# Softmax by small exponentials on ScalarE, and another order of the first batch, in a fused attention and expert kernel

## The chip, the cores and the metric

The kernel runs on one core of a Trainium2 chip. A core has a matrix engine (TensorE, PE in the profile), a vector engine (VectorE, DVE), an activation engine (ScalarE, ACT), a general engine (GpSimd, POOL) and SyncE (SP), which issues the DMAs. Each engine runs its own instructions in their order and waits for the others by semaphores. The metric is the device time of one execution in microseconds (us): 1990.22 before, the median of three runs (1989.96 to 1992.01).

## The reference

Three layers follow each other, all in float32. The change touches the first.

```python
def _attn_ref(q, k, v):                       # 4 batches, 8 heads, 576 rows, 64 wide
    k_p = k.reshape(B, H, 72, 8, D).mean(axis=3)
    v_p = v.reshape(B, H, 72, 8, D).mean(axis=3)
    scores = scale * np.matmul(q, k_p.transpose(0, 1, 3, 2))
    scores = scores - np.max(scores, axis=-1, keepdims=True)
    attn = np.exp(scores)
    attn = attn / (np.sum(attn, axis=-1, keepdims=True) + 1e-09)
    return np.matmul(attn, v_p)
# x: (2304, 512), the heads side by side
# _moe_ref:  8 experts, x -> relu(x @ w1[e]) @ w2[e], summed with weights P[:, e]
#            from x @ w_gate by 8 rounds of row and column normalisation
# _moe2_ref: (silu(x @ w_gate) * (x @ w_val)) @ w_out
```

## The kernel before

Products of float32 are made of three products of a high and a low part (`mm3`, L112): a high part is a copy by ScalarE, a low part the difference to it by VectorE or POOL. The attention stage takes the first 200 us or so; the experts and the gated layer fill the rest.

**Tiles.** The 576 rows of a batch are cut into five query tiles (four of 128 rows, one of 64), 20 in all. For each, `task_a` transposes the queries (TensorE, then a copy qT by ScalarE, L345), `task_b` makes the scores of 8 heads by 72 keys in a PSUM tile mps (four products, L353) and has VectorE take the maximum of each head (L359) and the difference of scores and maximum into a tile e (L360). `task_exp` is one exponential over all 576 columns by ScalarE (L367). `task_b2` sums each head (L373, VectorE), adds a small constant, inverts (L374, L375) and multiplies (L377, on POOL, for tiles 1 and 2 on VectorE). `task_c` transposes e and splits it into aTh (ScalarE, L405) and aTl (VectorE, L406). When two (or three) tiles of a batch are through, `task_d` multiplies them with the masked values vh and vl in two halves of four heads, each in its own mps tile, and splits the result into xh and xl (L421, L422).

**Keys and values.** Rows of eight are summed by VectorE or POOL. `key_blocks` copies the transposed keys into block form kbd, the upper half of the partitions by ScalarE, the lower half by the engine it is given. `task_v2` splits the values; `mask` multiplies them with a head mask, vh on POOL, vl on VectorE (L324).

**Expert units in the gaps.** As soon as 256 rows of x are there, nine units of the first expert group are queued (`group0_units`): four first-layer blocks (12 products into a PSUM tile hps, then a copy hh by ScalarE, L135, and a low part hl by VectorE, L136), one gate block, four second-layer units. `fill()` puts one of them into the order at hand.

**What sets the order.** It is written out by hand (L605 to L694): what stands in the code first is issued first on each engine. A loop step takes one tile: query tile i+3, a unit, `task_c(i)`, a unit, `task_b(i+2)`, a unit, `task_exp`, keys and values of the next batch, and at the end of a chunk `values(i)`. PSUM has eight banks: two for tiles y, two for tiles h (queries, first-layer and gate blocks), and two mps tiles of two banks each. A new tile waits until the tile that had its banks before is read. TensorE's first 16 products (`warm`) multiply the identity with itself and are not used.

Loads go out on SP in the order of the code. A key or value tile kv has five buffers (NKV), so the first batch's values wait until the first keys are summed.

## Time and profile before

| | |
|---|---|
| median of three runs | 1990.22 us |
| profiled execution, its own time | 1990.33 us |
| its span in the profile | 1988.6 us |
| PE busy | 1964.8 us (99%) |
| DVE busy | 1425.2 us (72%) |
| ACT busy | 885.1 us (45%) |
| POOL busy | 1305.7 us (66%) |

A row of a timeline or of the chain gives the start and the length in us; in square brackets stands how long the engine was idle before it and who released it. "x8" is the number of records; a float32 product that is not split has two of them. PEclk is the clock that TensorE was granted, as a share of its full 2.4 GHz.

### The profile page before, as it was taken

How to read it: one execution, taken by the hardware profiler on the slowest of the kernel's cores; microseconds unless marked ns; L12 is line 12 of the kernel's file. 1: busy time of each engine (PE TensorE's matmuls, PEld its weight loads, DVE VectorE, ACT ScalarE, POOL GpSimd, SP SyncE). 2: the span in 40 equal slices, each digit the busy share in tenths (PEclk: the TensorE clock that was granted, in tenths of full speed). 3: DMA queues.
4: the chain of work that ended last, by engine and by line, in shares of the span. 5: the costliest groups of instructions: out<-in, count | busy, mean ns of one | idle time of the engine just before them, and what ended most of it. 6: DMA issues, size and time to landing. Idle time of an engine off the chain costs nothing.

```text
span 1988.6 us, 31110 instructions
## 1 busy us (share of the span) xinstructions
PE 1964.8 (99%) x11067; PEld 1872.2 (94%) x11067; DVE 1425.2 (72%) x2258; ACT 885.1 (45%) x1707; POOL 1305.7 (66%) x1162
## 2 busy tenths in 40 slices
PE   8999999999999999999999999999999999999998
PEld 7899888999999899999999999999999999999997
DVE  7773868777777868777777788777776855656555
ACT  4453534444444443443444434444444554544542
POOL 5775567878888466867767667677675766445442
PEclk8999999999999999999999999999999999999999
DMA  6674677888888889988989889899988564544532
GB/s 180 190 212 117 196 283 266 308 305 296 314 305 308 309 307 315 333 304 307 315 307 312 299 305 332 313 309 313 309 318 289 174 238 149 200 160 138 179 139 85
DMA packets 217227, 513.82 MB, mean 258 GB/s; under 512 B 35472, under 2 KB 107760, under 8 KB 210928
## 3 DMA queue, kind: packets, MB, share of 16 engines
q1 hardware_dynamic: 212176, 496.10, 72.7%
q0 software_dynamic: 4896, 15.73, 2.9%
q8 instruction: 88, 1.44, 0.3%
q14 instruction: 67, 0.55, 0.1%
HBM read 360.73 MB, written 151.04 MB: 257 GB/s over the span
## 4 chain that ended last, share of the span: by engine, by line
PE 91%; DVE 4%; POOL 2%; issue 2%; ACT 1%; DMA 0%; SPq 0%; DVEq 0%; POOLq 0%; ACTq 0%
PE aps L116 8%; PE aps L114 8%; PE aps L115 8%; PE mbs L114 7%; PE mbs L115 7%; PE mbs L116 7%; PE yps L1157 6%; PE yps L1159 6%; PE yps L1158 6%; PE cps L114 4%; PE cps L116 4%; PE cps L115 4%; PE bps L114 2%; PE bps L115 2%; PE bps L116 2%
## 5 line engine op out<-in xcount | busy, mean ns | idle before, releaser
L1086 ACT COPY LF<-aps 128x384 f32<-128x384 f32 x378 | 181.3, 480 | 440.4 <-PE aps L116 438.4
L1318 POOL TENSOR_TENSOR LR<-LF,LR 128x384 fp32r<-128x384 f32 x240 | 260.6, 1108 | 173.3 <-ACT LR L1316 173.0
L114 PE MATMUL mbs<-LR 128*128 128x384 f32 x840 | 283.2, 337 | 0.0
L115 PE MATMUL mbs<-LR 128*128 128x384 f32 x840 | 282.5, 336 | 0.0
L1365 DVE TENSOR_TENSOR AC<-mbs,AC 128x768 f32<-128x768 f32 x196 | 187.2, 955 | 132.4 <-PE mbs L116 131.7
L116 PE MATMUL mbs<-LR 128*128 128x384 f32 x840 | 281.9, 336 | 0.0
L1157 PE MATMUL yps<-LR 128*128 128x512 f32 x576 | 225.7, 392 | 0.3 <-DVE AC L1417 0.3
L1159 PE MATMUL yps<-LR 128*128 128x512 f32 x576 | 225.1, 391 | 0.6 <-DVE LR L1600 0.6
L1158 PE MATMUL yps<-LR 128*128 128x512 f32 x576 | 224.6, 390 | 0.2 <-POOL LR L66 0.2
L835 POOL TENSOR_TENSOR LR<-praw,LR 128x512 fp32r<-128x512 f32 (+1 forms) x130 | 136.1, 1068 | 108.1 <-ACT LR L829 63.0
L835 POOL TENSOR_TENSOR LR<-sums,LR 128x1024 fp32r<-128x1024 f32 x65 | 158.8, 2444 | 68.3 <-ACT LR L829 68.3
L1331 POOL TENSOR_TENSOR LF<-LF 128x384 f32<-128x384 f32 x120 | 128.9, 1074 | 56.5 <-DVE LF L1485 44.8
L115 PEld LDWEIGHTS mbs<-LR 128*128 128x128 f32 x840 | 157.8, 188 | 0.0
L116 PEld LDWEIGHTS mbs<-LR 128*128 128x128 f32 x840 | 157.7, 188 | 0.0
L114 PEld LDWEIGHTS mbs<-LR 128*128 128x128 f32 x840 | 157.6, 188 | 0.0
L1419 DVE SCALAR_TENSOR_TENSOR AC<-yps,pr,AC 128x512 f32<-128x512 f32 x168 | 121.3, 745 | 30.7 <-PE yps L1159 27.0
L1325 ACT COPY LF<-bps 128x384 f32<-128x384 f32 x120 | 57.7, 481 | 185.3 <-DVE bps L1485 179.8
L1335 POOL TENSOR_TENSOR LF<-LF 128x384 f32<-128x384 f32 x120 | 130.5, 1088 | 9.4
L1159 PEld LDWEIGHTS yps<-LR 128*128 128x128 f32 x576 | 108.1, 188 | 24.5 <-DVE LR L1600 1.0
L1157 PEld LDWEIGHTS yps<-LR 128*128 128x128 f32 x576 | 108.2, 188 | 19.1 <-DVE AC L1417 0.7
L66 POOL TENSOR_TENSOR LR<-rraw,LR 128x512 fp32r<-128x512 f32 x72 | 99.2, 1399 | 41.0 <-ACT LR L65 36.6
L1158 PEld LDWEIGHTS yps<-LR 128*128 128x128 f32 x576 | 108.2, 188 | 18.4 <-POOL LR L66 0.7
(308 smaller groups left out, 5744.1 us busy)
## 6 DMA issues: line engine op xcount, KB each, us to landing
LR<-w1s_d SPq DMA_DIRECT2D x210, 512.0 KB
LR<-w2s_d SPq DMA_DIRECT2D x210, 512.0 KB
w1s_d<-LR SPq DMA_DIRECT2D x29, 1792.0 KB
w2s_d<-LR SPq DMA_DIRECT2D x24, 1024.0 KB
w2s_d<-LR SPq DMA_DIRECT2D x90, 256.0 KB
praw<-in_moe_w_dram SPq DMA_DIRECT2D x30, 512.0 KB
rraw<-in_moe_w_dram SPq DMA_DIRECT2D x30, 512.0 KB
LR<-rows_d POOLq DMA_DIRECT2D x12, 1024.0 KB, 7.0
```

The lines of the kernel that those rows point to most:

```text
L114: nc.tensor.matmul(ps, lhsT=wh, rhs=ah, start=start, stop=False, skip_group_check=more)
L115: nc.tensor.matmul(ps, lhsT=wh, rhs=al, start=False, stop=False, skip_group_check=more)
L116: nc.tensor.matmul(ps, lhsT=wl, rhs=ah, start=False, stop=stop, skip_group_check=more)
L835: nc.gpsimd.tensor_tensor(out=lo, in0=src, in1=hi.bitcast(F32), op=ALU.subtract)
L1086: nc.scalar.copy(out=t, in_=ps[:, :HB])
L1157: nc.tensor.matmul(ps, lhsT=hh[:, o:o + P], rhs=wh, start=j == 0, stop=False)
L1158: nc.tensor.matmul(ps, lhsT=hh[:, o:o + P], rhs=wl, start=False, stop=False)
L1159: nc.tensor.matmul(ps, lhsT=hl[:, o:o + P], rhs=wh, start=False, stop=j == 1)
L1318: eng.tensor_tensor(out=lo[:, c], in0=src[:, c], in1=hi[:, c].bitcast(F32), op=ALU.subtract)
L1331: nc.gpsimd.tensor_tensor(out=r_of(q, a), in0=r_of(q, b), in1=r_of(q, a), op=ALU.subtract)
L1335: nc.gpsimd.tensor_tensor(out=r_of(q, a), in0=r_of(q, a), in1=r_of(q, b), op=ALU.subtract)
L1365: nc.vector.tensor_tensor(out=acc_of(m), in0=ps[:, :, :HB], in1=acc_of(m), op=ALU.add)
```

## The change

The scores keep their PSUM tile. VectorE takes the negated maximum only. ScalarE runs one exponential for each head of a tile, eight of 72 columns, from PSUM, with the negated maximum as bias and the sum of the head as its accumulated output; the scale goes into the copy of the queries. The difference and the sum by VectorE are gone. In the loop the first four exponentials come before a unit and the other four behind it. The key blocks of the first batch are copied by columns: ScalarE both partition halves of the first two blocks, VectorE those of the last two. The first batch's values are loaded into the accumulator AC, which is not in use then. Its four masks are all made on POOL and stand before the transposes. Seven more unused products stand before the first transposes. The second half of the first chunk's value products goes to two y tiles instead of an mps tile. Tile 2 is normalised on POOL. The low parts of the first expert's weights are made in two instructions each.

```diff
@@ -98,8 +98,11 @@
             if kind == "col":
                 hi, lo = (a.rearrange("p (k f) -> p k f", k=KD) for a in (hi, lo))
             load_w(src + 1)
-            raw = raws[src]
-            split(raw[:, :, j * P:(j + 1) * P] if kind == "col" else raw[:, j, :], hi, lo)
+            raw = raws[src][:, :, j * P:(j + 1) * P] if kind == "col" else raws[src][:, j, :]
+            nc.scalar.activation(out=hi, in_=raw, func=AF.Copy)
+            for c in range(2):
+                h = (slice(None), slice(2 * c, 2 * c + 2)) if kind == "col" else (slice(None), slice(2 * P * c, 2 * P * c + 2 * P))
+                nc.gpsimd.tensor_tensor(out=lo[h], in0=raw[h], in1=hi[h].bitcast(F32), op=ALU.subtract)
             if j == 1:
                 load_w(src + 3)
             parts.append((hi, lo))
@@ -247,7 +250,10 @@
 
         flat = src[b].rearrange("h (j r) d -> (h j) (r d)", r=POOL)
         r = min(P, NK - c * P)
-        t = att.tile([P, POOL * D], F32, tag="kv", name="kv", bufs=NKV)
+        if src is v and b == 0:
+            t = AC[:, c * POOL * D:(c + 1) * POOL * D]
+        else:
+            t = att.tile([P, POOL * D], F32, tag="kv", name="kv", bufs=NKV)
         nc.sync.dma_start(out=t[:r], in_=flat[c * P:c * P + r])
         kv_t[src is k, b, c] = t
 
@@ -280,16 +286,16 @@
         r = min(P, NK - c * P)
         nc.tensor.transpose(flat[:, c * P:c * P + r], kp[:r, c].rearrange("p a d -> p (a d)"), ident[:r, :r])
 
-    def key_blocks(flat, second):
+    def key_blocks(flat, a, copy):
         keys = flat[:, 0:NK].rearrange("p (a b) -> p a b", a=NP)
-        nc.scalar.copy(out=kbd[0:D, :, 0:SP], in_=keys[0:D, :, 0:SP])
-        second(out=kbd[D:P, :, SP:2 * SP], in_=keys[D:P, :, SP:2 * SP])
+        copy(out=kbd[0:D, a, 0:SP], in_=keys[0:D, a, 0:SP])
+        copy(out=kbd[D:P, a, SP:2 * SP], in_=keys[D:P, a, SP:2 * SP])
 
     def task_k2(b):
         flat = m_tile().rearrange("p a b -> p (a b)")
         for c in range(NC):
             key_transpose(flat, c)
-        key_blocks(flat, nc.scalar.copy)
+        key_blocks(flat, slice(0, NP), nc.scalar.copy)
 
     def first_keys():
 
@@ -299,7 +305,8 @@
             if c == 3:
                 query(0)
             key_transpose(flat, c)
-        key_blocks(flat, nc.vector.tensor_copy)
+        key_blocks(flat, slice(0, 2), nc.scalar.copy)
+        key_blocks(flat, slice(2, NP), nc.vector.tensor_copy)
 
     vh = att.tile([P, 2, NP, 2, D], F32R, name="vh")
     vl = att.tile([P, 2, NP, 2, D], F32R, name="vl")
@@ -324,13 +331,13 @@
         eng.tensor_tensor(out=dst[:, s, :, a], in0=src[:, s:s + NP].to_broadcast([P, NP, 2 - s, D]),
                           in1=hmask[:, s, :, a].unsqueeze(3).to_broadcast([P, NP, 2 - s, D]), op=ALU.mult)
 
-    def task_v2(b):
+    def task_v2(b, eng=nc.vector):
 
         nc.scalar.activation(out=vp_h, in_=vp, func=AF.Copy)
         nc.vector.tensor_tensor(out=vp_l, in0=vp, in1=vp_h.bitcast(F32), op=ALU.subtract)
         for s in range(2):
             mask(nc.gpsimd, vh, vp_h.bitcast(F32), s)
-        return [lambda s=s: mask(nc.vector, vl, vp_l, s) for s in range(2)]
+        return [lambda s=s: mask(eng, vl, vp_l, s) for s in range(2)]
 
     qT, ex, aT = {}, {}, {}
 
@@ -342,7 +349,7 @@
             nc.tensor.transpose(ps[:, p * P:p * P + n],
                                 t[:n, 2 * p:2 * p + 2, :].rearrange("p a d -> p (a d)"), ident[:n, :n])
         qt = att.tile([P, NP, P], F32, tag="qT", name="qT", bufs=2)
-        nc.scalar.copy(out=qt[:, :, :n], in_=ps.rearrange("p (a t) -> p a t", a=NP)[:, :, :n])
+        nc.scalar.mul(out=qt[:, :, :n], in_=ps.rearrange("p (a t) -> p a t", a=NP)[:, :, :n], mul=1.0 / (POOL * D ** 0.5))
         qT[i] = qt
 
     def task_b(i):
@@ -356,24 +363,23 @@
         st = att.tile([P, 3, 2, 4, 1], F32, tag="st", name="st", bufs=3)
         e = e_bufs[i % 3]
         ev = e[:n, 0:NK].rearrange("p (a h j) -> p a h j", a=2, h=4)
-        nc.vector.tensor_reduce(out=st[:n, 0, :, :, 0], in_=sc, axis=AX.X, op=ALU.max)
-        nc.vector.tensor_tensor(out=ev, in0=sc, in1=st[:n, 0].to_broadcast([n, 2, 4, SP]), op=ALU.subtract)
-        ex[i] = (e, st)
-
-    def task_exp(i):
+        nc.vector.tensor_reduce(out=st[:n, 0, :, :, 0], in_=sc, axis=AX.X, op=ALU.max, negate=True)
+        ex[i] = (e, st, sc, ev)
+
+    def task_exp(i, which=(0, 1)):
         n = per[i][2]
-        e = ex[i][0]
-
-        nc.scalar.activation(out=e[:n, 0:NK], in_=e[:n, 0:NK], func=AF.Exp, scale=1.0 / (POOL * D ** 0.5))
+        e, st, sc, ev = ex[i]
+        for a in which:
+            for h in range(4):
+                nc.scalar.activation(out=ev[:, a, h], in_=sc[:, a, h], func=AF.Exp, bias=st[:n, 0, a, h, :],
+                                     accum_out=st[:n, 1, a, h, :])
 
     def task_b2(i):
         b, s, n = per[i]
-        e, st = ex[i]
-        ev = e[:n, 0:NK].rearrange("p (a h j) -> p a h j", a=2, h=4)
-        nc.vector.tensor_reduce(out=st[:n, 1, :, :, 0], in_=ev, axis=AX.X, op=ALU.add)
+        e, st, sc, ev = ex[i]
         nc.vector.tensor_scalar(out=st[:n, 1], in0=st[:n, 1], scalar1=EPS, scalar2=None, op0=ALU.add)
         nc.vector.reciprocal(out=st[:n, 2], in_=st[:n, 1])
-        eng = nc.vector if i in (1, 2) else nc.gpsimd
+        eng = nc.vector if i == 1 else nc.gpsimd
         eng.tensor_tensor(out=ev, in0=ev, in1=st[:n, 2].to_broadcast([n, 2, 4, SP]), op=ALU.mult)
 
     CH = [(0, 2), (2, TPB)]
@@ -396,7 +402,7 @@
         if key not in aT:
             aT[key] = [att.tile([P, NC, 320], F32R, tag=t, name=t, bufs=1) for t in ("aTh", "aTl")]
         ah, al = aT[key]
-        e, st = ex.pop(i)
+        e = ex.pop(i)[0]
         ps = m_tile()
         flat = ps.rearrange("p a b -> p (a b)")
         for c in range(NC):
@@ -409,17 +415,21 @@
     def task_d(b, c, half):
         s0, cn = chunk_rows(b, c)
         ah, al = aT[b, c]
-        ps = m_tile()
+        ps = [new_y().unsqueeze(1) for _ in range(2)] if b + c == 0 and half else [m_tile()]
         for pp in range(2):
             p = half * 2 + pp
+            y = ps[pp][:, 0, :cn] if len(ps) == 2 else ps[0][:, pp, :cn]
             for s in range(2):
                 wh = vh[:, s, p].rearrange("p a d -> p (a d)")
                 wl = vl[:, s, p].rearrange("p a d -> p (a d)")
-                mm3(ps[:, pp, :cn], wh, wl, ah[:, p + s, :cn], al[:, p + s, :cn], s == 0, s == 1)
+                mm3(y, wh, wl, ah[:, p + s, :cn], al[:, p + s, :cn], s == 0, s == 1)
         t0 = b * S + s0
-        dst = (slice(None), slice(half * 2, half * 2 + 2), slice(t0, t0 + cn))
-        nc.scalar.activation(out=xh[dst], in_=ps[:, :, :cn], func=AF.Copy)
-        nc.vector.tensor_tensor(out=xl[dst], in0=ps[:, :, :cn], in1=xh32[dst], op=ALU.subtract)
+        w = 2 // len(ps)
+        for i, y in enumerate(ps):
+            k = half * 2 + i * w
+            dst = (slice(None), slice(k, k + w), slice(t0, t0 + cn))
+            nc.scalar.activation(out=xh[dst], in_=y[:, :, :cn], func=AF.Copy)
+            nc.vector.tensor_tensor(out=xl[dst], in0=y[:, :, :cn], in1=xh32[dst], op=ALU.subtract)
 
 
     def task_gate(j):
@@ -617,13 +627,13 @@
         for c in range(NC - 1):
             task_v1(0, c)
         last_values()
+        warm(7)
         task_b2(0)
         task_b2(1)
-        masks.extend(task_v2(0))
+        for f in task_v2(0, nc.gpsimd):
+            f()
         task_c(0)
         task_c(1)
-        next_mask()
-        next_mask()
         query(2)
         split_w(2)
         query(3)
@@ -633,11 +643,11 @@
         task_exp(2)
         split_w(4)
         task_b2(2)
-        gate_weights()
         fill()
         query(4)
         task_b(3)
         fill()
+        gate_weights()
         task_exp(3)
         split_w(6)
         for bc in key_parts(3):
@@ -663,9 +673,10 @@
                     task_k2(t // TPB)
                     fill()
                 task_b(t)
+                task_exp(t, (0,))
                 fill()
                 next_mask()
-                task_exp(t)
+                task_exp(t, (1,))
             for bc in key_parts(t):
                 task_k1(*bc)
             for bc in value_parts(i):
```

ScalarE in the first batch, from the key blocks to the split of the values; first before, then after.

```order
L285 COPY kbd<-mps 64x4x72
L345 COPY qT<-qps 128x512
L367 ACTIVATE e_110<-e_110 128x576
L367 ACTIVATE e_111<-e_111 128x576
L320 COPY vp<-yps 128x64
L329 ACTIVATE vp_h<-vp 128x320
```

```order
L291 COPY kbd<-mps 64x2x72
L292 COPY kbd<-mps 64x2x72
L352 ACTIVATE qT<-qps 128x512
L374 ACTIVATE e_110,st<-mps,st 128x72 x8
L374 ACTIVATE e_111,st<-mps,st 128x72 x8
L327 COPY vp<-yps 128x64
L336 ACTIVATE vp_h<-vp 128x320
```

Two exponentials have become sixteen, which read the scores (mps) and the maxima (st) and write the sums into st; two key copies of half the columns stand where one stood.

TensorE at the same place, from the scores of tiles 0 and 1 to those of tile 2; first before, then after.

```order
L353 MATMUL mps<-kbd,qT 128x144 x8
L318 MATMUL yps<-kv,ident 128x64 x8
L403 MATMUL mps<-ident,e_110 128x128 x5
L403 MATMUL mps<-ident,e_111 128x128 x5
L342 MATMUL qps<-ident,q 128x128 x8
L353 MATMUL mps<-kbd,qT 128x144 x4
```

```order
L360 MATMUL mps<-kbd,qT 128x144 x8
L325 MATMUL yps<-AC,ident 128x64 x8
L613 MATMUL mps<-ident 128x128 x7
L409 MATMUL mps<-ident,e_110 128x128 x5
L409 MATMUL mps<-ident,e_111 128x128 x5
L349 MATMUL qps<-ident,q 128x128 x8
L360 MATMUL mps<-kbd,qT 128x144 x4
```

The seven unused products stand between the sum of the last values and the transposes of tile 0.

ScalarE in the loop at tile 7 (its exponentials write e_111), where first-layer copies hh surround them; first before, then after.

```order
L135 ACTIVATE hh<-hps 128x256
L405 ACTIVATE aTh<-mps 128x5x128
L135 ACTIVATE hh<-hps 128x256 x2
L367 ACTIVATE e_111<-e_111 128x576
L345 COPY qT<-qps 128x4x64
L135 ACTIVATE hh<-hps 128x256
```

```order
L138 ACTIVATE hh<-hps 128x256
L411 ACTIVATE aTh<-mps 128x5x128
L138 ACTIVATE hh<-hps 128x256
L374 ACTIVATE e_111,st<-mps,st 128x72 x4
L138 ACTIVATE hh<-hps 128x256
L374 ACTIVATE e_111,st<-mps,st 128x72 x4
L352 ACTIVATE qT<-qps 128x4x64
L138 ACTIVATE hh<-hps 128x256
```

The copy hh that stood before the exponential now stands behind four of the eight.

## Rows read from the trace of the kernel before

**Rows 1.** The page, busy time: us, share of the span, instructions
```profile
PE 1964.8 (99%) x11067; PEld 1872.2 (94%) x11067; DVE 1425.2 (72%) x2258; ACT 885.1 (45%) x1707; POOL 1305.7 (66%) x1162
```

**Rows 2.** Windows of TensorE: from:to, length, busy (instructions), granted clock, DMA share, GB/s
```profile
17.00:18.00 1.00, 0.06 (x1) 1.00 1.16 231
...
18.00:19.00 1.00, 0.00 (x0) 0.52 0.34 64
...
24.00:25.00 1.00, 1.00 (x6) 0.57 0.39 94
```

**Rows 3.** Waits of TensorE, 30 to 260 us: sum, times, longest
```profile
PE hps L114 <- DVE hl L136: 2.9, 4, 1.1
```

**Rows 4.** Chain of waits, 10 to 28 us: start, length, what
```profile
10.77 0.47 DVE kbd L286
...
11.28 2.30 PE mps L353 x8
...
13.61 0.77 DVE st L359
...
17.62 0.20 DVE st L375
...
19.42 1.33 DVE e L377
...
20.88 1.31 PE mps L403 x5
...
23.77 2.03 DVE vl L324 x2
```

**Rows 5.** Timeline of TensorE: start, length, instruction, idle before and releaser
```profile
25.25 0.38 PE L114 MATMUL mps<-aTh,vh 128*128 128x256 f32 x1
...
27.41 0.36 PE L114 MATMUL mps<-aTh,vh 128*128 128x256 f32 x1 [0.46 <-DVE e L360]
...
30.47 0.38 PE L115 MATMUL hps<-xl,wh 128*128 128x256 f32 x1 [0.34 <-DVE xl L422]
...
32.64 0.38 PE L114 MATMUL hps<-xh,wh 128*128 128x256 f32 x1
...
54.24 0.42 PE L114 MATMUL mps<-aTh,vh 128*128 128x320 f32 x1 [0.81 <-DVE aTl L406]
```

**Rows 6.** ScalarE by line and shape, whole run: busy, mean ns, idle before
```profile
L367 ACT ACTIVATE e<-e 128x576 f32<-128x576 f32 x16 | 10.9, 683 | 16.0 <-DVE e L360 15.8
...
L65 ACT ACTIVATE wh<-raw 128x512 fp32r<-128x512 f32 x8 | 4.6, 621 | 0.0
...
L894 ACT ACTIVATE pr<-pr,small 128x144 f32<-128x144 f32 x1 | 0.4, 418 | 0.6 <-DVE small L893 0.6
...
L320 ACT COPY vp<-yps 128x64 f32<-128x64 f32 x1 | 0.2, 193 | 0.0
```

**Rows 7.** VectorE by line and shape, 0 to 200 us
```profile
L360 DVE TENSOR_TENSOR e<-mps,st 128x576 f32<-128x576 f32 x16 | 12.1, 758 | 0.6
...
L373 DVE TENSOR_REDUCE st<-e 128x8 f32<-128x576 f32 x16 | 11.9, 742 | 0.3
```

**Rows 8.** Timeline of ScalarE, two splits back to back
```profile
23.55 1.15 ACT L65 ACTIVATE wh<-raw 128x512 fp32r<-128x512 f32 x2
```

**Rows 9.** Timeline of POOL, end of the first value sums
```profile
16.63 0.32 POOL L263 TENSOR_TENSOR vp<-kv 128x64 f32<-128x64 f32 x1
```

**Rows 10.** Timelines of VectorE, ScalarE, TensorE at two later places
```profile
64.14 0.74 DVE L359 TENSOR_REDUCE st<-mps 128x8 f32<-128x576 f32 x1
...
64.96 0.38 ACT L135 ACTIVATE hh<-hps 128x256 fp32r<-128x256 f32 x1 [2.02 <-PE hps L116]
...
66.06 0.39 PE L114 MATMUL hps<-xh,wh 128*128 128x256 f32 x1 [0.75 <-DVE hl L136]
...
137.02 0.76 DVE L359 TENSOR_REDUCE st<-mps 128x8 f32<-128x576 f32 x1 [0.21 <-PE mps L353]
...
139.43 0.31 PE L114 MATMUL mps<-aTh,vh 128*128 128x320 f32 x1
```


## The prediction

> **What bounds the kernel now.** I read the busy times first: TensorE is busy 99% of the span [rows 1], so a change pays only where TensorE stands still or runs slowly. The windows of one microsecond show where that is. At 17 us TensorE stops, at 18 us its granted clock has fallen to half (0.52; of the two levels, 1.2 instead of 2.4 GHz), and it stays low until about 25 us [rows 2]. After that hardly anything is lost: from 30 to 260 us the longest sum of TensorE's waits is 2.9 us, for VectorE's low parts hl (L136) [rows 3]. So everything the change can win lies in the first 55 us or so, and what it can lose lies in all 200 us of the attention stage, because there each new wait of TensorE is paid in full.
>
> Then the chain of waits through the first batch [rows 4]. VectorE copies its half of the key blocks after ScalarE has copied the other, and the score products start at 11.28. VectorE then takes maxima, differences and sums of two tiles alone, and its last normalisation (L377) starts at 19.42; TensorE transposes tile 1 at 20.88. VectorE's masks of the low values come at 23.77, after all that. In TensorE's order of time the value products start at 25.25, have a gap of 0.46 at 27.41 (the second half wants a score tile that VectorE has not finished) and one of 0.34 at 30.47; the second first-layer block starts at 32.64 and the second chunk's value products at 54.24, after a wait of 0.81 [rows 5].
>
> **The price of one small exponential.** Before, a tile costs ScalarE one exponential of 0.683 us and VectorE a difference of 0.758 and a sum of 0.742 [rows 6, 7]. After, VectorE saves these 1.50 us, and ScalarE runs eight exponentials of 72 columns, with a bias read per partition and an accumulated sum. No row has that shape. The only one with such a bias is L894: 0.418 us for 144 columns [rows 6]. A column costs (0.621 - 0.193) / (512 - 64) = 0.00096 us by two rows without bias, so 72 columns fewer make 0.35 us for one alone. Back to back they overlap: two of L65 take 1.15 us where one takes 0.621, so the second adds 0.53, 0.09 less than its duration [rows 6, 8]. That leaves 0.26; the scores come from PSUM, and L320, a PSUM row of 64 columns, takes 0.193 [rows 6], which lets me go down by some hundredths. I take 0.24 each, 1.92 a tile, with nothing added for the accumulated sum. The bounds are 0.11 (the PSUM row with 8 columns more, less the overlap, the bias free) and 0.35 (the bias row without overlap, if each exponential must hand over its sum before the next begins).
>
> The Trainium skill speaks against the change here: "ScalarE: Activation LUTs", section "Rules for kernel authors", says to budget about 0.3 us for an ACTIVATE with a pointer bias and 0.83 ns per element more, 0.36 us for this shape. The overlap of the L65 pair says that a row of instructions is cheaper than that, but no run here shows one with an accumulator. By the page's figure, as an estimate, a tile costs 2.9 us and the sum below comes out near 2001 instead of 1991.
>
> **The change, part by part.**
>
> *Key blocks in halves by columns.* Two of tile 0's four score products need only ScalarE's part and run beside VectorE's copies. The four take 2.30 us [rows 4]; two are 1.1, less some 0.4 for the smaller copies: -0.7.
>
> *First softmax chain.* The maximum of tile 0 ends at 13.61 + 0.77 - 0.70 = 13.68. Sixteen exponentials of 0.24 end at 17.52. VectorE adds the small constant and inverts (two small instructions of 0.2, with the gap 0.45), and normalises tile 1, 1.0 (between L360's 0.76 and L377's own 1.33) [rows 4, 7]. The transposes start 0.14 later, at 19.1 instead of 20.88: -1.8 together with the key blocks.
>
> *Seven warm-up products.* They fill TensorE from about 16.4 to 18.2, where it stood still, so the clock should not fall at 18 us. From 20.88 to 25.25 TensorE worked 4.4 us at the low clock [rows 2, 5]; at the full one the transposes, queries and scores take about 2.2, but ScalarE's copies between them hold them at 2.9: -1.5. If the clock falls all the same, these 1.5 us stay lost. The products themselves cost nothing as long as tile 0's normalisation is not ready before 18.1; it is not, since POOL's value sums end at 17 [rows 9] and the normalisation, no cheaper than VectorE's 1.0, comes behind them.
>
> *Masks before transposes, all four on POOL.* The high values come from ScalarE at 18.2 and POOL needs 2.1 us for each pair (VectorE's pair took 2.03 [rows 4]): ready at 22.4, where the value products would otherwise start at 22.0, but only their later ones need the last mask: +0.2.
>
> *Second value half in two other PSUM tiles, tile 2 normalised by POOL.* The gap of 0.46 goes, and of the 0.6 us that the first layer lost around 30.47 most goes with halves of the copy: -1.0. Up to here -1.8 - 1.5 + 0.2 - 1.0 = -4.1 at 31 us.
>
> *What gives it back at once.* ScalarE works in order. Behind tile 2's exponentials stand two splits, a copy hh and the query copy that frees the PSUM bank of the second first-layer block (32.64 [rows 5]). They were 0.6 us and are 1.92: +1.3, and -2.8 remains. The same queue repeats at tile 3 and tile 5, but there it replaces waits for VectorE (the longest one for hl, 1.1 us, and the 0.81 at 54.24 [rows 3, 5]), so I count these as even.
>
> *What it costs later.* Two kinds of place. First, half the exponentials now stand in front of the copy hh of the first-layer block that runs after the scores. Before, at 64.96 hh ran at once and the difference of VectorE made hl wait; after, the maximum (64.14 + 0.74) is followed by 4 x 0.24, hh (0.38), hl (0.42) and the semaphores, so the block at 66.06 starts near 66.8: +0.75 [rows 10]. The next first-layer block uses the same bank, so nothing hides it. Three more tiles have this order (maxima at 88.49, 105.31 and 129.90; +0.35, +0.6, +0.35). Second, the scores stay in their PSUM tile until the last exponential, where the difference took them out in 0.76. The second value half takes that tile. At 137.02 the maximum starts; 0.76, eight exponentials and a logit copy of 0.3 between them end near 140.1, and TensorE wanted the tile at 139.43 [rows 10]: +0.65. The other chunk ends by the same sum: 0.3, 0.2 and 0.55, and nothing at 95 us. Together 2.05 + 1.7 = +3.7.
>
> *At no cost.* Low parts split in two instructions on POOL (TensorE waits for none of them in this stretch); scaling the query copy (same instruction); the gate's weights later (the first gate block comes two first-layer blocks behind). The values of the first batch go to the accumulator's space, so SP is not held for free key tiles and its weight loads go out earlier; POOL's sums, not the loads, set the values, so I put it at nothing, within 1 us either way, because the first queries share the queue. VectorE's 1.5 us a tile after 60 us free an engine that TensorE does not wait for.
>
> **Sum.** -4.1 + 1.3 + 3.7 = +0.9 us. The profiled execution's own time is 1990.33 (span 1988.6), 0.1 above the median of the three runs, so 1991.1 against the median of 1990.22. What can be told from no change is 0.2%, 4 us.
>
> **Rivals.**
> - *The exponentials are cheap* (0.16, between 0.11 and my value): the exponentials end at 16.24, and POOL's masks hold the value products to 21.1 (-4.1 with the clock); gaps -1.0, the queue gives back 0.7, the places after 60 us shrink to 0.9, and the 1.1 us wait for hl goes as well. -4.6: 1985.6. For it speaks the short PSUM row of 0.193; against it that the row has neither bias nor accumulator.
> - *ScalarE becomes the bound* (0.35, no overlap). The chain is 16 x 0.35 = 5.6 us, the transposes of tile 1 start at 20.9 as now, TensorE idles and the clock falls as now; gaps -1.0, the queue +2.2, the eight places 3.7 + 0.11 x 48 = +9.0 (each hundredth costs four places 0.04 and four 0.08). +10.2: 2000.4. It decides from about 0.28 on: a hundredth costs 0.16 in the first chain, 0.08 in the queue and 0.48 later, 0.72 together, and the sum passes +4. For it: the only bias row. Against: the overlap of the L65 pair.
> - *The clock falls anyway*, because TensorE waits again between the two transposes: +1.5, 1992.6, within no change.
> - *The change does not relieve what binds*: POOL's four masks, one behind the other, hold the value products where VectorE's hold them now, the start comes out even and the places after 60 us stay: +3.7, 1993.9.
>
> **Chances.** Forecast with its neighbours (price 0.17 to 0.28, with either state of the clock, and the fourth rival) 0.38, its own range 1986.3 to 1994.2. Cheap exponentials, or later waits that other work hides, 0.33. ScalarE as the bound 0.29. So faster by over 0.2% 0.33, within 0.38, slower 0.29. The range is 1984 to 1999.5: it leaves out a bit of either end, the price of 0.35 above all.
>
> **What would show it.** The row of the small exponentials (start to start 0.24); TensorE's transposes of tile 1 at 19.1, value products near 22, first-layer block near 25; a granted clock of 1.0 from 15 to 26 us; TensorE waiting for ScalarE's hh or exponentials at the eight places, in place of VectorE. It is wrong if a spacing above 0.28 or below 0.17 shows, if the clock is low for as long as before, or if TensorE shows no new waits for ScalarE between 60 and 160 us.

## The result and the profile after

The changed kernel takes **2001.56 us** (median of 6 runs, 2000.73 to 2005.38) where the kernel before took 1990.21 (6 runs): ratio 1.0057, 95% interval 1.0047 to 1.0068, 11.3 us slower. The forecast was 1991.1 and its range ended at 1999.5. The span in the profile grew by 11.2 us, from 1988.6 to 1999.8.

The page's busy times, beside [rows 1]: VectorE has lost 35 us, ScalarE has gained 36, and TensorE's share has gone from 99% to 98%.

```profile
PE 1966.8 (98%) x11081; PEld 1872.5 (94%) x11081; DVE 1390.0 (70%) x2217; ACT 920.8 (46%) x2009; POOL 1310.1 (66%) x1173
```

The price of a small exponential stands in ScalarE's timeline (start, length, instruction, idle before and releaser), at the first tile:

```profile
12.89 0.32 ACT L374 ACTIVATE e<-mps,st 128x72 f32<-128x72 f32 x1 [1.67 <-DVE st L366]
13.11 0.19 ACT L374 ACTIVATION_READ_ACCUMULATOR e<-mps,st 128x1 f32 x1
13.21 0.31 ACT L374 ACTIVATE e<-mps,st 128x72 f32<-128x72 f32 x1
...
13.50 0.32 ACT L374 ACTIVATE e<-mps,st 128x72 f32<-128x72 f32 x1
```

The accumulated sum is an instruction of its own behind each exponential. From start to start a pair takes some 0.295 us (0.29 between 13.21 and 13.50; fifteen steps of e2, from 13.55 to 17.99, give 0.296), so a tile holds ScalarE's queue for 8 x 0.295 = 2.36 us.

The windows of TensorE (from:to, length, busy, granted clock, DMA share, GB/s), beside [rows 2]: the fall of the clock at 18 us is gone, and there is a new one at 51 us. Before, there was also an earlier fall, from 11 to 15 us, that the prediction does not mention; this execution of the changed kernel does not have it. First before, then after:

```profile
12.00:13.00 1.00, 1.00 (x6) 0.50 0.70 144
```

```profile
12.00:13.00 1.00, 1.00 (x9) 1.00 1.09 267
...
18.00:19.00 1.00, 0.50 (x5) 1.00 0.02 4
...
51.00:52.00 1.00, 0.47 (x2) 0.51 1.05 186
52.00:53.00 1.00, 1.00 (x6) 0.50 1.02 360
```

TensorE's waits from 30 to 260 us (sum, times, longest). Before, only the second of these rows was there, with 2.9 us [rows 3], and one of 0.5 for the gate block (gps). The sums of the five rows have grown by 14 us.

```profile
PE mps L117 <- ACT e L374: 5.6, 6, 1.4
PE hps L117 <- DVE hl L139: 4.5, 4, 1.6
PE hps L117 <- ACT qT L352: 4.0, 3, 1.4
PE mps L360 <- ACT e L374: 2.2, 1, 2.2
...
PE gps L439 <- DVE hl L139: 1.1, 1, 1.1
```

The chain through the first batch (start, length, what), beside [rows 4]: the scores of tile 0 now take 1.43 where the same four products took 2.30, and sixteen exponentials fill the time from the maximum to the values.

```profile
10.65 1.43 PE mps L360 x8
...
12.10 0.77 DVE st L366
...
12.89 4.95 ACT e L374 x32
...
19.25 0.73 PE mps L409 x5
```

TensorE's timeline shows where the waits are, beside [rows 5, 10]:

```profile
22.23 0.38 PE L117 MATMUL mps<-aTh,vh 128*128 128x256 f32 x1
...
29.79 0.39 PE L117 MATMUL hps<-xh,wh 128*128 128x256 f32 x1 [1.32 <-ACT qT L352]
...
51.53 2.29 PE L360 MATMUL mps<-kbd,qT 128*128 128x144 f32 x8 [2.19 <-ACT e L374]
...
57.30 0.42 PE L117 MATMUL mps<-aTh,vh 128*128 128x320 f32 x1 [1.38 <-ACT e L374]
...
68.23 0.38 PE L117 MATMUL hps<-xh,wh 128*128 128x256 f32 x1 [1.61 <-DVE hl L139]
...
88.26 0.39 PE L117 MATMUL hps<-xh,wh 128*128 128x256 f32 x1 [1.26 <-ACT qT L352]
```

Value products start at 22.23 (25.25 before) and the second first-layer block at 29.79 (32.64): 2.9 us are won in this execution (e6 and e10 below, with the same first batch, start their value products at 23.17 and 23.80). From 51 us on they are lost, in steps of 0.3 to 2.2 us. As marks along the way serve the copies xh, one at the end of each half chunk, in ScalarE's timeline. First before, then after:

```profile
58.06 0.70 ACT L421 ACTIVATE xh<-mps 128x640 fp32r<-128x640 f32 x1 [1.05 <-PE mps L116]
...
173.68 0.70 ACT L421 ACTIVATE xh<-mps 128x640 fp32r<-128x640 f32 x1 [1.05 <-PE mps L116]
```

```profile
59.37 0.70 ACT L431 ACTIVATE xh<-mps 128x640 fp32r<-128x640 f32 x1 [1.53 <-PE mps L119]
...
184.88 0.70 ACT L431 ACTIVATE xh<-mps 128x640 fp32r<-128x640 f32 x1 [1.05 <-PE mps L119]
```

The lead of 2.9 us at 48 us is a lag of 1.3 at 59 us (+4.2) and of 11.2 at 185 us (+9.9). The lag of the mark at 168.46 is 11.2 too; nothing is lost behind it.

### The profile page after: what moved, and what is told of

Same layout as the page of the kernel before. It is cut to its first block, busy times and chain, and to the rows that moved or that the text cites. A ratio compares the mean times of both kernels' runs of the same rounds, so it can differ in the third digit from the quotient of the medians.

```text
span 1999.8 us, 31411 instructions
## 1 busy us (share of the span) xinstructions
PE 1966.8 (98%) x11081; PEld 1872.5 (94%) x11081; DVE 1390.0 (70%) x2217; ACT 920.8 (46%) x2009; POOL 1310.1 (66%) x1173
## 4 chain that ended last, share of the span: by engine, by line
PE 90%; ACT 3%; DVE 3%; DMA 1%; issue 1%; POOL 0%; SPq 0%; DVEq 0%; ACTq 0%; POOLq 0%
PE aps L119 8%; PE aps L117 8%; PE aps L118 8%; PE mbs L117 7%; PE mbs L118 7%; PE mbs L119 7%; PE yps L1168 6%; PE yps L1170 6%; PE yps L1169 6%; PE cps L119 4%; PE cps L117 4%; PE cps L118 4%; PE bps L117 2%; PE bps L119 2%; PE bps L118 2%; ACT e L374 2%
```

## The experiments

All are timed against the kernel before on the same chip (median 1990.55 us in the first four, 1990.43 in the next four, 1989.99 in the last); each row of marks and waits is from one profiled execution.

**e1 and e2: the change without its softmax, and with it in the first two tiles only.** What the new softmax does for a tile, it does only if the tile's number is in SMALL; otherwise maximum, difference, one exponential and sum stand where they stood before.

```diff
+    SMALL = ()            # e1;   e2: (0, 1)
...
+        if i not in SMALL:
+            nc.vector.tensor_tensor(out=ev, in0=sc, in1=st[:n, 0].to_broadcast([n, 2, 4, SP]), op=ALU.subtract)
...
+            if 1 in which:
+                nc.scalar.activation(out=e[:n, 0:NK], in_=e[:n, 0:NK], func=AF.Exp)
...
+            nc.vector.tensor_reduce(out=st[:n, 1, :, :, 0], in_=ev, axis=AX.X, op=ALU.add)
```

> The changed kernel with the softmax of before in all 20 tiles (difference and sum by VectorE, one exponential), every other part of the change kept. Theory Q (the small exponentials fill ScalarE's queue; every other part is a gain or nothing): the loss is gone and a part of the first batch's gain stays. The changed kernel ran its second first-layer block 2.9 us earlier than before; without the sixteen exponentials the first chain is a little different, so 1986 to 1988. Rival R (the other parts cost too, such as four masks on POOL or three copies of x in the first chunk): 1991 or more.

> Small exponentials for tiles 0 and 1 alone, the softmax of before for the other 18, all else as in the changed kernel. Theory Q: the value products start as early as in the changed kernel (first x copy at 23.9 us against 27.0 before) and nothing gives it back: query transposes of tile 4 near 26.8, then 3 to 4.5 us kept, 1986 to 1987.5, and at or below the kernel with the old softmax everywhere. Rival S (the first chain gains from the order and the warm clock alone, not from the exponentials): the same as with the old softmax within 0.5 us, or slower.

e1: **1986.15 us**, 0.9977 (0.9969 to 0.9986); e2: 1986.22, 0.9978 (0.9969 to 0.9986). Without the new softmax the change is 4.4 us faster than the kernel before on the same chip, and the softmax costs 2001.56 - 1986.15 = 15.4 us. And it does not pay in the first chain either, where it was to start the transposes earlier: e2 is no faster than e1, as its rival S had it. The marks of e1, against those of after above:

```profile
53.88 0.70 ACT L440 ACTIVATE xh<-mps 128x640 fp32r<-128x640 f32 x1 [1.05 <-PE mps L119]
...
169.48 0.70 ACT L440 ACTIVATE xh<-mps 128x640 fp32r<-128x640 f32 x1 [1.05 <-PE mps L119]
```

After lags e1 by 5.5 us at the first and by 15.4 at the second. These two profiled executions differ by 16.8 us in all (1984.69, the fastest of e1's, and 2001.53), so nearly all of it lies in the attention stage.

**e3: the new softmax alone in the kernel before.**

```diff
-        nc.vector.tensor_reduce(out=st[:n, 0, :, :, 0], in_=sc, axis=AX.X, op=ALU.max)
-        nc.vector.tensor_tensor(out=ev, in0=sc, in1=st[:n, 0].to_broadcast([n, 2, 4, SP]), op=ALU.subtract)
+        nc.vector.tensor_reduce(out=st[:n, 0, :, :, 0], in_=sc, axis=AX.X, op=ALU.max, negate=True)
...
+                nc.scalar.activation(out=ev[:, a, h], in_=sc[:, a, h], func=AF.Exp, bias=st[:n, 0, a, h, :],
+                                     accum_out=st[:n, 1, a, h, :])
```

> The kernel before with the new softmax alone (scaled queries, negated maximum, eight exponentials with accumulator, four in front of the unit), nothing else of the change. Theory Q: the later places cost what they cost in the changed kernel (13.5 to 14 us from its lead of 2.9 us at 48 us to its lag of 11.2 at 168 us) and the first batch's gain is missing: 2002 to 2006. Rival R: at most 1998.

2006.73 us, 1.0079 (1.0066 to 1.0093), 16.2 slower and 0.7 above the expectation: about the same loss on the other base, so the two parts of the change add up (16.2 - 4.4 = 11.8 against 11.3 measured).

**e4: no accumulated sum.** The eight exponentials without accum_out; VectorE sums as before.

```diff
-                nc.scalar.activation(out=ev[:, a, h], in_=sc[:, a, h], func=AF.Exp, bias=st[:n, 0, a, h, :],
-                                     accum_out=st[:n, 1, a, h, :])
+                nc.scalar.activation(out=ev[:, a, h], in_=sc[:, a, h], func=AF.Exp, bias=st[:n, 0, a, h, :])
...
+        nc.vector.tensor_reduce(out=st[:n, 1, :, :, 0], in_=ev, axis=AX.X, op=ALU.add)
```

> The changed kernel without the accumulated sums: eight exponentials with a bias, then the sum by VectorE as before. ScalarE's start to start should fall from 0.295 to 0.20 us, so 0.76 us a tile. Theory Q, with the slope of the prediction (0.72 us for a hundredth): -6.8 us, about 1995; by the measured loss in proportion to the queue (13.5 us for 2.36 - 0.58 us a tile) -5.8 us, about 1996. Rival P (it is the place of the exponentials in front of the copies and in the score tile, whatever they cost): 1999 or more.

1993.3 us, 1.0016 (1.0007 to 1.0025): 8.3 us less than the changed kernel, where 5.8 to 6.8 were expected. ScalarE's timeline at the first two tiles:

```profile
14.39 3.53 ACT L374 ACTIVATE e<-mps,st 128x72 f32<-128x72 f32 x16 [2.43 <-DVE st L366]
17.77 0.27 ACT L327 COPY vp<-yps 128x64 f32<-128x64 f32 x1
```

(17.77 - 14.39) / 16 = 0.211 us each. So bias, PSUM and 72 columns cost 0.21; the accumulated sum adds 0.084, and 8.3 us to the time, though VectorE has its sums back.

**e5 and e9: ScalarE's queue alone.** e1 with unused exponentials that have bias and accumulator, four before the unit and two behind it, and then the one real exponential. VectorE's difference frees the scores' PSUM tile as before, 1.5 us after the maximum begins (3.2 to 5.5 us in the changed kernel).

```diff
+    idle = att.tile([P, SP + 1], F32, name="idle")
...
+            for a in which if i > 1 else ():
+                for h in range(2 if a else 4):
+                    nc.scalar.activation(out=idle[:n, 0:SP], in_=ident[:n, 0:SP], func=AF.Exp, bias=st[:n, 0, a, h, :],
+                                         accum_out=idle[:n, SP:SP + 1])
```

```diff
-                    nc.scalar.activation(out=idle[:n, 0:SP], ...
-                                         accum_out=idle[:n, SP:SP + 1])
+                    nc.scalar.activation(out=idle[(4 * a + h) % 3][:n], ...
+                                         accum_out=idle_sums[:n, a, h])      # e9: three bf16 tiles in turn, eight sums
```

> The old softmax with all other parts of the change (1986.15 us in the first experiment), and from tile 2 on six unused exponentials of 72 columns with bias and accumulator before the tile's one exponential, four of them in front of the unit's copy. ScalarE's queue is then as long as in the changed kernel (6 x 0.295 + 0.58 = 2.36 us a tile), but they read and write SBUF, so that the scores leave their PSUM tile with VectorE's difference, as before. Theory 'both': the queue costs the growth of TensorE's waits for hl and qT, some 6 us: 1992 to 1993, and the rest of the 15.4 us is the PSUM tile that the exponentials hold. Rival 'queue': ScalarE's time alone makes the loss: 1999 to 2001. Rival 'tile': the held PSUM tile alone makes it: 1986 to 1987.5.

> The fifth experiment again with outputs that differ: six unused exponentials of 72 columns a tile write three tiles in turn and sums of their own (bf16, for want of space), where before each wrote over the one ahead and started 0.48 us after it. Theory 'rewriting makes the 0.48, and the queue decides': the exponentials stand 0.28 to 0.32 apart, the queue is 2.3 to 2.5 us a tile as in the changed kernel, and the time is 1996 to 2000, most of the 15.4 us, without a held PSUM tile. Rival 'source': reading SBUF makes the 0.48, and the time stays near 2009. Rival 'both': 1992 to 1994, the held tile being the rest.

e5 took 2009.77 us, 1.0094 (1.0081 to 1.0108), outside all three expectations, since the queue was longer than meant. ScalarE's timelines of e5 and of e9:

```profile
53.00 0.35 ACT L379 ACTIVATE idle<-ident,st 128x72 f32<-128x72 f32 x1 [3.11 <-DVE st L368]
...
53.48 0.36 ACT L379 ACTIVATE idle<-ident,st 128x72 f32<-128x72 f32 x1
```

```profile
50.27 0.35 ACT L380 ACTIVATE idle<-ident,st 128x72 bf16<-128x72 f32 x1 [3.10 <-DVE st L369]
...
50.63 0.34 ACT L380 ACTIVATE idle<-ident,st 128x72 bf16<-128x72 f32 x1
...
50.97 0.34 ACT L380 ACTIVATE idle<-ident,st 128x72 bf16<-128x72 f32 x1
```

0.48 us from start to start in e5, 0.34 in e9 (0.36 for the first step). With that e9's queue is 6 x 0.34 + 0.59 = 2.6 us a tile, a little above the 2.36 of the changed kernel, and it takes **2001.73 us**, 1.0057 (1.0045 to 1.0070): as much as the changed kernel, with no tile held. That is 1.7 above the range of its own theory; its rival "source" (near 2009) falls. TensorE's waits in e9, and one of its windows:

```profile
PE hps L117 <- DVE hl L139: 5.4, 4, 1.9
PE hps L117 <- ACT qT L355: 4.5, 3, 1.5
PE mps L117 <- DVE aTl L427: 3.2, 1, 3.2
```

```profile
58.00:59.00 1.00, 1.00 (x6) 0.50 0.00 0
```

The waits for e are gone; those for hl and qT are 20% and 13% above those of the changed kernel, and one for aTl has come (by the order of the instructions the sum of VectorE stands behind the longer queue here, and normalisation and transposes behind the sum). But the equal time is made up of other losses. I compared the starts of the same products in two traces, from the first value products to 185 us. Against e1 the changed kernel loses 16.6 us: 4.7 at the waits for qT, 2.8 at those for hl and 9.5 where exponentials hold a PSUM tile (with the low clock behind 51 us), less 0.4 elsewhere. e9 loses 15.7: 5.3 at qT, 3.9 at hl, 2.2 at aTl, 0.3 elsewhere, and 4.0 because the clock is low for ten microseconds (54 to 61 and 71 to 75 us). So e9 shows that the queue alone, with VectorE's old work behind it, can cost this much. It does not show that the queue makes the whole loss of the changed kernel: "tile" falls, as the time without a held tile is nowhere near 1987, and "both" stands.

**e6: all eight exponentials behind the unit.**

```diff
-                task_exp(t, (0,))
                 fill()
                 next_mask()
-                task_exp(t, (1,))
+                task_exp(t)
```

> The changed kernel (2001.56 us) with all eight exponentials of a tile behind the unit, where the one exponential stood before. Theory 'the PSUM tile and the queue': the waits for hl fall by 1.6 us, the tile is held half a unit's copy longer at seven or eight places (+0.5 each): 2002 to 2004. Rival 'place': four exponentials in front of hh are the main cost: under 1997.

2000.87 us, 1.0049 (1.0035 to 1.0062): outside both expectations, 0.7 below the changed kernel. TensorE's waits:

```profile
PE hps L117 <- ACT qT L352: 4.5, 4, 1.5
...
PE hps L117 <- DVE hl L139: 2.1, 4, 0.5
```

The waits for hl fall from 4.5 to 2.1, those for qT rise by 0.5, and the clock is low later and for as long (3.4 us, from 54 to 57). Where the queue stands hardly matters.

**e8: the score tile held longer, the queue short.** e1 with VectorE's difference behind unit and mask.

```diff
-        if i not in SMALL:
+        if i < 2:
             nc.vector.tensor_tensor(out=ev, in0=sc, in1=st[:n, 0].to_broadcast([n, 2, 4, SP]), op=ALU.subtract)
...
             if 1 in which:
+                if i > 1:
+                    nc.vector.tensor_tensor(out=ev, in0=sc, in1=st[:n, 0].to_broadcast([n, 2, 4, SP]), op=ALU.subtract)
```

> The old softmax with all other parts of the change, VectorE's difference of tiles 2 and on moved behind the unit and the mask, so that the scores hold their PSUM tile longer while ScalarE's queue stays short. Theory 'the held tile costs by itself': TensorE's waits for mps tiles come back in part, up to the 7.8 us that they sum to in the changed kernel: 1988 to 1994. Rival 'queue': 1986 to 1987.5.

1990.71 us, 1.0000 (0.9992 to 1.0009), 4.6 above e1, but not by the wait it was meant to bring. TensorE's waits:

```profile
PE hps L117 <- ACT qT L353: 2.5, 3, 1.0
...
PE mps L117 <- DVE e L378: 0.6, 2, 0.3
```

The later difference delays the exponential, and the query copy behind it in ScalarE's queue is late. The edit also held the tile longer in only eight tiles (2.5 to 4.3 us from the maximum on; 1.5 in e1). The changed kernel waits for e behind tiles 5, 6, 8, 11, 13, 16 and 18; of these only 13 and 18 are held longer in e8, and behind each of them TensorE waits 0.3. So the 0.6 is the price at two of seven places, and not that of holding a tile in general.

**e10: the old softmax in tiles 3, 4 and 5 of the changed kernel.**

```diff
-    SMALL = ()
+    SMALL = (0, 1, 2, *range(6, 20))
```

> The changed kernel with the old softmax in tiles 3, 4 and 5 alone. By the landmarks of the traces (changed kernel against the first experiment) the loss between 25 and 54 us is 6.7 us, the one after it 8 to 10. Theory 'place by place': 2001.6 - 6.7 = 1994 to 1996, and TensorE's clock doesn't fall at 51 us. Rival 'the later places take it up again' (they were hidden behind the early loss): over 1998.

1999.16 us, 1.0043 (1.0030 to 1.0055), 2.4 below the changed kernel: a miss. The clock is 1.00 from 50 to 56 us, as expected. But the second value half waits all the same:

```profile
55.28 0.41 PE L117 MATMUL mps<-aTh,vh 128*128 128x320 f32 x1 [1.20 <-ACT e L381]
```

That wait is for tile 6, and the wait for qT at 30 us is tile 2's. Lined up product by product against e1, the changed kernel loses 6.7 us between the first value products and the second value half, e10 3.1: the three tiles' part was 3.6. The time shows 2.4; e10's profiled execution also starts its value products 1.6 us later than that of the changed kernel, with nothing changed ahead of them. The later places did not take it up (the changed kernel and e10 both lose 9.9 us against e1 between their marks at 57 to 59 and 183 to 185 us): the expectation had put their neighbours' cost on them.

**e7, e11 and e12: parts of the first batch taken out of e1.** e7: without the seven unused products; e11: masks of the low values on VectorE behind the transposes and tile 2 normalised by VectorE; e12: the second value half in one mps tile.

```diff
-        warm(7)                                                      # e7
...
-        for f in task_v2(0, nc.gpsimd):                              # e11
-            f()
+        masks.extend(task_v2(0))
         task_c(0)
         task_c(1)
+        next_mask()
+        next_mask()
...
-        eng = nc.vector if i == 1 else nc.gpsimd                     # e11
+        eng = nc.vector if i in (1, 2) else nc.gpsimd
...
-        ps = [new_y().unsqueeze(1) for _ in range(2)] if b + c == 0 and half else [m_tile()]
+        ps = [m_tile()]                                              # e12
```

> The old softmax with all other parts of the change but the seven unused products. Theory: they keep the clock up between the score products and the transposes, and are worth the 1.5 us of the prediction: 1987.6. Rival: with the old softmax the clock falls at 17 us with them too (0.50 from 17 to 20 us), so they are worth nothing: 1985.7 to 1986.6.

> The old softmax with all other parts of the change (1986.15 us), but masks of the low values by VectorE behind the transposes, and tile 2 normalised by VectorE, as before. Theory of the prediction (masks on POOL cost 0.2, tile 2's normalisation has no part in it): 1985.5 to 1986.7. Rival 'the order of the masks is what the change gains by': 1987.5 to 1989.

> The old softmax with all other parts of the change (1986.15 us), but the second half of the first chunk's value products in one score tile, as before. Theory of the prediction (the gap of 0.46 and most of 0.6 us come back): 1986.8 to 1987.6. Rival (other work fills the gap by now): 1985.5 to 1986.6.

e7: 1987.74 us, 0.9986 (0.9977 to 0.9995), 1.6 above e1. e11: 1986.13, 0.9979 (0.9970 to 0.9988), no difference. e12: 1987.76, 0.9988 (0.9980 to 0.9997), 1.6 above e1. The intervals of e7 and e12 overlap with e1's. The windows of TensorE around the transposes, e1 and then e7:

```profile
17.00:18.00 1.00, 1.00 (x6) 0.50 1.24 261
...
20.00:21.00 1.00, 1.00 (x10) 1.00 0.00 0
```

```profile
22.00:23.00 1.00, 1.00 (x6) 0.50 0.00 0
```

The clock falls in both; with the unused products it is back at 20 us, without them between 23 and 24. These are single executions: e5, e8 and e9 have the first batch of e1, and in theirs the clock stays at 1.00 there.

## Why the prediction was wrong

**The price failed first.** The step "I take 0.24 each, 1.92 a tile, with nothing added for the accumulated sum" is wrong by the sum: 0.211 without it (e4, within 0.03 of what I took), 0.295 with it. By the prediction's own slope of 0.72 us a hundredth that makes 5.5 x 0.72 = 4.0 us. Its own limit (0.28) was passed, so the second rival, ScalarE as the bound with 2000.4 us, is what came. Its total fits, its reasons only in part: its price was 0.35, and it let the first chain gain nothing and the clock fall at 18 us.

The Trainium skill ("ScalarE: Activation LUTs", section "Rules for kernel authors") gave 0.36 us for this shape and, by my estimate, a time near 2001. The trace's mean duration of such an exponential is 0.336, but what counts in a queue, start to start, is 0.295 with the sum read out and 0.211 without. The agreement of the total is not one of the price.

**Tiles 3 to 5 failed.** The step "there it replaces waits for VectorE, so I count these as even" holds for the waits it names: the longest, 1.1 for hl [rows 3], became 0.49 at 32.40, and the 0.81 for aTl [rows 5] is gone. Tile 3's queue brings a wait of its own, 1.37 for qT at 36.01, but a wait for key copies (0.46 at 46.32 before) is gone too, and the lead is 2.9 us at 30 us and at 48. But in the stretch from 48 to 59 us 4.2 us are lost. The scores of tile 6 find their PSUM tile held by tile 5's exponentials (2.19 at 51.53), TensorE stands still, the clock falls to 0.5 for three microseconds (the scores take 2.29 where 1.25 is usual), and the second value half waits 1.38 for tile 6. Held tiles I had looked for at the chunk ends only, not for the next scores.

**The later places were mis-sized.** Forecast +3.7, measured +9.9 between the marks. The four hh places were right but for the price: the waits grew by 0.86, 0.64, 0.68 and 0.64, 2.8 in all, where 2.05 was forecast and the price adds 4 x 0.04 x 5.5 = 0.9. The chunk ends (0.88, 0.34, 0.86, 1.02 and 1.14 us) make 4.2, where 1.7 was forecast and the price adds 4 x 0.08 x 5.5 = 1.8; the 0.34, at 104 us, is the one put at nothing. The query copy qT behind the exponentials, which the prediction follows at tile 2 only, comes again at 88.26: 1.26 not counted. These make 8.3 us of waits. The other 1.6 are at the new waits as well: the starts of the products, before and after, fall apart by some 0.26 us more than the listed wait at each of the six places where there was no wait before (five chunk ends and the query copy), and by no more than it at the four hh places, which waited before too. At 76.03, one of the six, it looks like this:

```profile
76.03 0.39 PE L117 MATMUL mps<-aTh,vh 128*128 128x256 f32 x1 [0.88 <-ACT e L374]
76.25 0.28 PE L118 MATMUL mps<-aTl,vh 128*128 128x256 f32 x1
```

The next product starts 0.22 behind the first where 0.12 is usual, and the listed wait begins only when the record of the last product before it ends, 0.28 after its start.

Tiles 3 to 5 and the later places make the whole error of 10.4 us: 4.2 + 6.2.

**The first batch came out right, partly by chance.** Transposes of tile 1 at 19.23 (19.1 forecast), value products at 22.23 (22.0), clock 1.00 at 18 us, a lead of 2.9 us at 48 us (2.8). But from the first maximum to those transposes it was 20.88 - 13.61 = 7.27 us before [rows 4] and is 19.23 - 12.10 = 7.13: the small exponentials give 0.1, not 1.1. What carried the number came ahead of that maximum, which begins 1.5 us earlier. From the start of the scores to the maximum it is 1.45 us instead of 2.33, and that is the clock: before, it was at 0.50 from 12 to 14 us, and the prediction took the 2.30 of [rows 4] as the price of the four products, with no word of the clock. e10 has the key halves too, with the clock at 0.50 there, and needs 2.32. The scores follow the last key transposes by 0.92 us instead of 1.25, 0.3 from the key halves where 0.7 was forecast, and in this execution the last key transposes begin 0.3 earlier (9.73 instead of 10.03). e1 and e2 agree: with or without small exponentials there, the time is the same. The warm products were sized right (1.5 forecast, 1.6 by e7), the y tiles low (1.0, 1.6 by e12), the masks as good as right (+0.2, 0.0 by e11).

**Why ScalarE binds at 46% busy.** It is no matter of its total. At 66 us, in ScalarE's timeline of the changed kernel:

```profile
66.13 0.32 ACT L374 ACTIVATE e<-mps,st 128x72 f32<-128x72 f32 x1 [1.88 <-DVE st L366]
...
67.33 0.39 ACT L138 ACTIVATE hh<-hps 128x256 fp32r<-128x256 f32 x1
...
68.78 0.43 ACT L352 ACTIVATE qT<-qps 128x256 f32<-128x256 f32 x1
```

It stands idle for 1.88 us until the maximum is there, and then all that it has to do comes at once: hh starts at 67.33, 1.2 us behind the first exponential, where before it ran the moment its product was done [rows 10]. Every microsecond of queue behind the maximum costs about as much in each variant: over e1 with its 0.59 us a tile, e4 pays 7.2 us for 1.1 more, e9 15.6 for 2.0, the changed kernel 15.4 for 1.8, e5 23.6 for 2.9: 6.5 to 8.7 us each, with 9 forecast (0.72 for 0.08). So the slope was about right, and the zero point was not. e4's VectorE has its sums, e5's and e9's their differences too, and the clock is low for some ten microseconds in these two, so these are no clean doses.

What stays open: how the loss divides between the queue and the held PSUM tiles. In the changed kernel's trace 7.5 of 16.6 us are lost at the waits for hl and qT and 9.5 where a tile is held (0.4 is won elsewhere), but both come from the same exponentials. e9 takes the hold away and loses as much by other waits and a low clock; e8 lengthens it at two of the seven places only. No run shortens the hold with nothing else changed. Of the 4.4 us that e1 gains, e7 and e12 give 3.2; the key halves were not tried alone, and e1's trace does not have the low clock at 12 us either, which e4 and e10 show with the same key halves.

**The better version** is e1, 1986.15 us: the change without its softmax, 0.2% below the kernel before (interval 0.14 to 0.31%).

## What to carry to other kernels

Price a run of small instructions by the step from start to start, count what each one issues, and treat an accumulated output as one more instruction until a trace shows otherwise. An engine that is half idle can still be the bound if it works in order and waits for the same event as the work behind it: then ask for each thing queued behind the new work who waits for it, at every tile, not at the one where one happened to look. A buffer that the new work holds longer must be followed to everyone who takes it next.

## What had not been expected of the hardware

The accumulated output of an ACTIVATE shows as an ACTIVATION_READ_ACCUMULATOR, 0.19 us long at the start of a row and 0.29 at the end of sixteen; it adds 0.084 us from start to start. In a row of sixteen pairs (e2, first two tiles, ScalarE's timeline) the durations grow while the steps stay the same:

```profile
13.55 0.32 ACT L381 ACTIVATE e<-mps,st 128x72 f32<-128x72 f32 x1 [1.67 <-DVE st L367]
...
13.86 0.31 ACT L381 ACTIVATE e<-mps,st 128x72 f32<-128x72 f32 x1
...
17.70 0.40 ACT L381 ACTIVATE e<-mps,st 128x72 f32<-128x72 f32 x1
...
17.99 0.41 ACT L381 ACTIVATE e<-mps,st 128x72 f32<-128x72 f32 x1
```

0.30 apart at either end, though one takes 0.32 and the other 0.40: the mean duration (0.336) is no price. And exponentials that write over the output of the one ahead started 0.48 us apart (e5), those with outputs of their own 0.34 (e9, in bf16, so that the type has changed with it).
